# Decode attention with a dense branch on one core: loaded tiles at multiples of 512 bytes, the output sum in four column groups of one bank, and a store in quarter rows

## The chip, the core and the metric

One Trainium2 chip, one of its cores. The metric is the device time in microseconds (us), median of several executions. Executions of one kernel mostly agree within 0.3%, and all that are compared here are of the state "fast" (the one exception, a single look at a kernel that only loads, is marked). The profile's span, from first to last instruction, is about 2 us shorter than the time.

Names in the profiles: PE multiplies matrices and PEld loads its weights; DVE, ACT and POOL are the vector, scalar and general engines; SP issues DMAs (SPq and ACTq are issues by SP and ACT). The inputs lie in HBM, the tiles in SBUF with 128 partitions, the sums of PE in banks of PSUM. The granted clock is the share of full clock that PE was given. A landing is the moment when a DMA's semaphore reports that all of it has arrived.

## The reference, cut to what matters

For two sequences, one token each (`x` is 2x448), the kernel computes `x + attention(layernorm(x)) + mlp(layernorm(x))`.

```python
# attention: 16 query heads, 8 kv heads, head size 256, the last W = 4096 keys of a cache
scores = einsum("bhqd,bhkd->bhqk", q, k[:, :, Sk - W:]) * 256 ** -0.5
o      = einsum("bhqk,bhkd->bhqd", softmax(scores), v[:, :, Sk - W:])   # then @ wo (4096x448)
# mlp: h = xn @ w1 + b1 (448x1792); h * tanh(softplus(h)) @ w2 (1792x448)
```

For each pair of sequence and kv head, 2 MB of K and 2 MB of V are read and used once: 77.66 MB in all with the weights.

## The kernel before: what the change and the argument touch

```python
consts = ctx.enter_context(tc.tile_pool(name="consts", bufs=1))   # small tiles first
wo_pool, k_pool, v_pool, kt_pool = ...                            # 3 x 3,584 B; 4 and 5 x 16,384 B; 3 x 8,192 B a partition
# all the loads below go through one queue, nc.sync, K two heads ahead
nc.sync.dma_start(out=t[:], in_=A_k_cache[b, kvh, s0:Sk, :].rearrange("(p t) d -> p (t d)", p=P))
...
psA = [ps_a.tile([Bsz, DO], FP32, name=f"psA{n}") for n in range(NO)]     # NO = 2 banks, DO = 224
def add(n, lhsT, rhs, **flags):                                          # the sum of all branches
    nc.tensor.matmul(psA[n][:, :], lhsT=lhsT, rhs=rhs, skip_group_check=True, **flags)
...
for n in range(NH):                                                      # softmax denominators, fp32
    nc.tensor.matmul(den[:], lhsT=rs[:, n:n+1].to_broadcast([P, P]), rhs=hsel[:], ...)
...
load_v(i, parts=1 if i < NK - 1 else 2)     # the last V in two halves, then wo in two halves
...
res = consts.tile([Bsz, D], BF16)
nc.vector.tensor_copy(out=res[:, 0:DO], in_=psA[0][:, :])
nc.scalar.copy(out=res[:, DO:D], in_=psA[1][:, :])
nc.sync.dma_start(out=out.flatten_outer_dims(), in_=res[:])
```

After the last V part has landed, `values` multiplies it (a pair of weight load and matmul for each 128x128 block of V), `oT` is scaled, and `mix` multiplies it by wo into `psA`. I call that last `mix` the last product.

The softmax here doesn't subtract the row's maximum and nothing guards it: scores larger than these inputs give would overflow.

## Time and profile before

| | before |
|---|---|
| time | 194.92 us (194.56 to 195.1, 3 runs) |
| span of the profiled run | 192.7 us |
| PE, weight loads, DVE busy | 68%, 42%, 53% of the span |
| read from HBM | 77.67 MB, 403 GB/s over the span |
| last V half lands | 187.2 us |
| from there to the end | 5.5 us |

Read it from the bottom: for 187 us the transfers set the time, then comes a tail that no transfer hides. The prediction below shows the lines.

### The profile page before, as it was taken

The page shows a single profiled execution, that of the slowest core. Times are in us where ns is not written, and L with a number is a line of the kernel's source. Part 1 is how long each engine was busy: PE and PEld are TensorE (multiplying, and loading weights), DVE is VectorE, ACT ScalarE, POOL GpSimd, SP SyncE. Part 2 cuts the span into 40 slices and gives each one's busy share as a digit, 9 for nine tenths or more (in the row PEclk, how much of TensorE's full clock was granted, in tenths as well). Part 3 has the DMA queues.
Part 4 walks back from the last instruction along what each step waited for, and adds up shares of the span by engine and source line. Part 5 has one row for each costly group of instructions (what it writes and reads, how often), then busy time and mean ns, then how long its engine had stood idle before and what let it go on. Part 6 is the DMA issues. An engine that isn't in the chain of part 4 may idle for free.

```text
span 192.7 us, 3810 instructions
## 1 busy us (share of the span) xinstructions
PE 130.4 (68%) x1624; PEld 81.3 (42%) x1624; DVE 102.2 (53%) x137; ACT 25.5 (13%) x69; POOL 24.8 (13%) x138
## 2 busy tenths in 40 slices
PE   0242993999827985499709881797449592898854
PEld 0142381466513654246504651364324452364752
DVE  4605506996638390929264753838091744748101
ACT  5000110112200211012200220021101110021100
POOL 7004320022110112002200210020200200000000
PEclk9999996699995799669975998599957979589965
DMA  6999999999999999999999999999999999999960
GB/s 211 424 447 408 427 427 435 428 435 402 431 422 428 425 415 428 435 418 414 429 425 432 420 416 430 428 425 411 428 432 428 403 434 422 432 414 429 410 253 2
DMA packets 7674, 77.90 MB, mean 404 GB/s; under 512 B 741, under 2 KB 2793, under 8 KB 3050
## 3 DMA queue, kind: packets, MB, share of 16 engines
q1 hardware_dynamic: 7652, 77.66, 96.1%
q8 instruction: 12, 0.20, 0.4%
q14 instruction: 4, 0.03, 0.0%
q10 hardware_dynamic: 6, 0.01, 0.0%
HBM read 77.67 MB, written 0.00 MB: 403 GB/s over the span
## 4 chain that ended last, share of the span: by engine, by line
DMA 96%; PE 1%; SPq 1%; issue 0%; ACT 0%; DVE 0%
DMA v<-in_A_v_cache_dram 51%; DMA k<-in_A_k_cache_dram 18%; DMA wo<-in_A_wo_dram 17%; DMA v<-in_B_w_dram 10%; PE psA L201 1%; PE o L411 1%; SPq L109 0%; SPq L325 0%; ACT res L484 0%; DVE oT L422 0%; SPq L336 0%
## 5 line engine op out<-in xcount | busy, mean ns | idle before, releaser
L352 DVE STREAM_TRANSPOSE kt<-k 128x2048 f32<-128x2048 f32 x32 | 73.5, 2300 | 48.9 <-DMA k<-in_A_k_cache_dram 48.9
L364 PE MATMUL sc<-kt,qdiag 128*128 128x512 bf16 x256 | 75.0, 443 | 14.4 <-DVE kt L352 14.3
L364 PEld LDWEIGHTS <-qdiag 128*128 128x128 bf16 x256 | 26.1, 111 | 50.5 <-issue 24.1
L374 ACT ACTIVATE p<-sc 128x512 bf16<-128x512 f32 x32 | 19.1, 597 | 144.8 <-PE sc L364 140.9
L244 POOL COPY qdiag<-qrep 32x8 bf16<-32x8 bf16 x128 | 21.0, 186 | 125.3 <-PE sc L364 109.8
L201 PE MATMUL psA<-wo,oT 128*2 128x224 bf16 x64 | 12.5, 370 | 31.3 <-DVE oT L422 31.3
L411 PEld LDWEIGHTS <-v 128*128 128x128 bf16 x1024 | 27.9, 97 | 6.3 <-DMA v<-in_A_v_cache_dram 3.0
L411 PE MATMUL o<-pT,v 128*128 128x2 bf16 x1024 | 28.1, 163 | 2.7 <-DMA v<-in_A_v_cache_dram 2.7
L385 DVE STREAM_TRANSPOSE pT<-p 128x512 bf16<-128x512 bf16 x32 | 21.4, 671 | 0.0
L201 PEld LDWEIGHTS <-oT 128*2 128x2 bf16 x64 | 6.5, 111 | 34.6 <-DVE oT L422 32.0
L393 PEld LDWEIGHTS den<-hsel,rs 128*128 128x128 f32 x64 | 11.7, 227 | 3.8 <-issue 2.1
L401 DVE RECIPROCAL rec<-den 128x2 f32<-128x2 f32 x16 | 2.5, 153 | 18.7 <-PE den L393 18.7
L393 PE MATMUL den<-hsel,rs 128*128 128x2 f32 x64 | 9.4, 252 | 0.0
L215 PE MATMUL qT_ps<-xs,v 128*128 128x4 bf16 x112 | 3.3, 166 | 6.1 <-DMA v<-in_A_wq_dram 6.1
L422 DVE TENSOR_TENSOR oT<-o,rec 128x4 bf16<-128x4 f32 x16 | 2.1, 134 | 8.5 <-PE o L411 8.5
L374 ACT ACTIVATION_READ_ACCUMULATOR p<-sc 128x1 f32 x32 | 6.2, 194 | 0.0
L215 PEld LDWEIGHTS <-v 128*128 128x128 bf16 x112 | 3.1, 104 | 6.6 <-DMA v<-in_A_wq_dram 6.6
L224 DVE CAST qT<-qT_ps 128x64 bf16<-128x64 f32 x1 | 0.2, 225 | 7.0 <-PE qT_ps L215 7.0
L169 PE MATMUL xnT_ps<-ident,xn_bf 2*128 2x2 bf16 x7 | 0.5, 166 | 5.0 <-DVE xn_bf L133 5.0
L270 PE MATMUL hT_ps<-xs,v 128*128 128x4 bf16 x49 | 3.7, 195 | 0.0
L270 PEld LDWEIGHTS <-v 128*128 128x128 bf16 x49 | 3.2, 149 | 0.3
L201 PE MATMUL psA<-v,act_bf 128*2 128x224 bf16 x28 | 2.8, 259 | 0.0
(40 smaller groups left out, 22.5 us busy)
## 6 DMA issues: line engine op xcount, KB each, us to landing
k<-in_A_k_cache_dram SPq DMA_DIRECT2D x16, 2048.0 KB, 32.5
v<-in_A_v_cache_dram SPq DMA_DIRECT2D x15, 2048.0 KB, 34.8
v<-in_B_w_dram SPq DMA_DIRECT2D x2, 1568.0 KB, 21.2
wo<-in_A_wo_dram SPq DMA_DIRECT2D x7, 448.0 KB, 31.8
v<-in_A_wq_dram SPq DMA_DIRECT2D x1, 2048.0 KB, 7.8
v<-in_A_v_cache_dram SPq DMA_DIRECT2D x2, 1024.0 KB, 29.9
v<-in_A_wq_dram SPq DMA_DIRECT2D x1, 1536.0 KB, 11.1
wo<-in_A_wo_dram SPq DMA_DIRECT2D x2, 224.0 KB, 24.1
```

The lines of the kernel that those rows point to most:

```text
L201: nc.tensor.matmul(psA[n][:, :], lhsT=lhsT, rhs=rhs, skip_group_check=True, **flags)
L215: nc.tensor.matmul(qT_ps[:, hh, e, :], lhsT=wq_v[s][:, hh, e, :], rhs=xs[:, s, :, :].rearrange("p x b -> p (x b)"), start=(s == 0), stop=( ...
L244: nc.gpsimd.tensor_copy(out=tv[rows, :, e, j * Q : j * Q + rep], in_=qrep[rows, :, h0 : h0 + rep, e, x, b],)
L270: nc.tensor.matmul(hT_ps[:, c, :, :].rearrange("p x b -> p (x b)"), lhsT=w1_v[:, s, c, :], rhs=xs[:, s, :, :].rearrange("p x b -> p (x b)" ...
L352: nc.vector.transpose(out=kt[:].bitcast(FP32), in_=k[:, half * TH * Dh : (half + 1) * TH * Dh].bitcast(FP32),)
L364: nc.tensor.matmul(psc[:], lhsT=qdiag[i % NW][:, n * NE + e, :], rhs=ktv[:, n, e, :, :], start=(n == 0 and e == 0), stop=(n == NB - 1 and ...
L374: nc.scalar.activation(out=p_sb[:], in_=psc[:].rearrange("p t c -> p (t c)"), func=ACT.Exp, scale=scale, accum_out=state["rs", i][:, s % N ...
L385: nc.vector.transpose(out=pT[:], in_=p_t.pop(s)[:])
L393: nc.tensor.matmul(den[:], lhsT=rs[:, n : n + 1].to_broadcast([P, P]), rhs=hsel[:], start=(n == 0), stop=(n == NH - 1),)
L401: nc.vector.reciprocal(out=state["rec", i][:], in_=den[:])
L411: nc.tensor.matmul(po[:, c, :], lhsT=vv[:, t, c, :], rhs=pTv[:, th, 0:rep], start=(t == 0 and c == 0), stop=(t == T - 1), skip_group_check ...
L422: nc.vector.tensor_tensor(out=oT[:, :, :, b], in0=po[:], in1=state.pop(("rec", i))[:].unsqueeze(1).to_broadcast([P, ND, rep]), op=ALU.mult,)
```

## The change

It has four parts. (1) The big pools stand right after two small tiles (`hsel` is widened for it) that together end at a multiple of 512 bytes, so every loaded tile starts at a multiple of 512 in its partition instead of at 96 modulo 256. The aim is cheaper transfers. (2) The sum runs in four column groups of 32 columns of the PE array, each with a quarter of the 448 output columns, in one bank; one copy takes it out; two queues store it as quarter rows. The aim is a shorter tail. (3) The denominators use a constant matrix of ones, after two small DVE instructions. (4) The last V comes as a half and two quarters.

```diff
-    consts = ctx.enter_context(tc.tile_pool(name="consts", bufs=1))
+    lead = ctx.enter_context(tc.tile_pool(name="lead", bufs=1))
+    ident = lead.tile([P, P], BF16)
+    hsel = lead.tile([P, Q], FP32)
     wo_pool = ...   # k_pool, v_pool, kt_pool
+    consts = ctx.enter_context(tc.tile_pool(name="consts", bufs=1))
@@
-    psA = [ps_a.tile([Bsz, DO], FP32, name=f"psA{n}") for n in range(NO)]   # NO = 2
+    psA = ps_a.tile([P, DO], FP32, name="psA")                              # NO = 4, DO = 112
+    def add(lhsT, w, start=False, stop=False):
+        for n in range(NO):
+            nc.tensor.matmul(psA[n * Q : n * Q + Bsz, :], lhsT=lhsT,
+                rhs=w[:, n * DO : (n + 1) * DO], start=start, stop=stop,
+                tile_position=(0, n * Q), skip_group_check=True)
@@
-        for n in range(NH):
-            nc.tensor.matmul(den[:], lhsT=rs[:, n : n + 1].to_broadcast([P, P]), rhs=hsel[:], ...)
+        nc.vector.tensor_scalar(out=sums[:], in0=hsel, scalar1=rs[:, 0:1], ...)
+        nc.vector.scalar_tensor_tensor(out=sums[:], in0=hsel, scalar=rs[:, 1:2], in1=sums[:], ...)
+        nc.tensor.matmul(den[:], lhsT=ones_f[:], rhs=sums[:], start=True, stop=True)
@@
-            load_v(i, parts=1 if i < NK - 1 else 2)
+            load_v(i, (0, T) if i < NK - 1 else (0, T // 2, 3 * T // 4, T))
@@
-    res = consts.tile([Bsz, D], BF16)
-    nc.vector.tensor_copy(out=res[:, 0:DO], in_=psA[0][:, :])
-    nc.scalar.copy(out=res[:, DO:D], in_=psA[1][:, :])
-    nc.sync.dma_start(out=out.flatten_outer_dims(), in_=res[:])
+    res = consts.tile([P, DO], BF16)
+    nc.vector.tensor_copy(out=res[:], in_=psA[:])
+    for b, queue in zip(range(Bsz), (nc.sync, nc.scalar)):
+        queue.dma_start(out=out[b].rearrange("s (n d) -> (s n) d", n=NO), in_=res[b : P : Q, :])
```

More of the change, by code (lines that the diff above doesn't have):

```diff
@@ L110 @@
         wq_sb += [w[:, s, :] for s in range(hi - lo)]
-    ident = consts.tile([P, P], BF16)
     make_identity(nc, ident[:])
@@ L152 @@
             )
-    hsel = consts.tile([P, rep], FP32)
-    nc.vector.tensor_copy(out=hsel[:], in_=ident[:, 0:rep])
+    hsel = hsel[:, 0:rep]
+    nc.vector.tensor_copy(out=hsel, in_=ident[:, 0:rep])
     for j in range(1, NQ):
         nc.vector.tensor_tensor(
-            out=hsel[:], in0=hsel[:], in1=ident[:, j * Q : j * Q + rep], op=ALU.add
+            out=hsel, in0=hsel, in1=ident[:, j * Q : j * Q + rep], op=ALU.add
         )
+    ones_f = consts.tile([P, P], FP32)
+    nc.gpsimd.memset(ones_f[:], 1.0)
     NW = 3
@@ L193 @@
     nc.vector.memset(ones[:], 1.0)
-    NO = 2
+    NO = NQ
     DO = D // NO
-    psA = [ps_a.tile([Bsz, DO], FP32, name=f"psA{n}") for n in range(NO)]
-    def add(n, lhsT, rhs, **flags):
-        nc.tensor.matmul(psA[n][:, :], lhsT=lhsT, rhs=rhs, skip_group_check=True, **flags)
-    for n in range(NO):
-        add(n, ident[0:Bsz, 0:Bsz], x_bf[:, n * DO : (n + 1) * DO], start=True, stop=False)
+    psA = ps_a.tile([P, DO], FP32, name="psA")
+    def add(lhsT, w, start=False, stop=False):
+        for n in range(NO):
+            nc.tensor.matmul(
+                psA[n * Q : n * Q + Bsz, :],
+                lhsT=lhsT,
+                rhs=w[:, n * DO : (n + 1) * DO],
+                start=start,
+                stop=stop,
+                tile_position=(0, n * Q),
+                skip_group_check=True,
+            )
+    nc.vector.memset(psA[:], 0.0)
+    add(ident[0:Bsz, 0:Bsz], x_bf[:, :], start=True)
     qrep = consts.tile([P, NB, HH, NE, NX, Bsz], BF16)
@@ L307, in dense_out @@
             for c in range(NF):
-                for n in range(NO):
-                    add(
-                        n,
-                        act_bf[:, c, x, :],
-                        w2_sb[:, x, c, n * DO : (n + 1) * DO],
-                        start=False,
-                        stop=False,
-                    )
+                add(act_bf[:, c, x, :], w2_sb[:, x, c, :])
     NSTEP = len(heads) * NH
@@ L328, in load_k, with load_v @@
         k_t[i] = t
-    def load_v(i, parts=1):
+    def load_v(i, cuts=(0, T)):
         kvh, b = heads[i]
@@ L333, in load_v @@
         vin = A_v_cache[b, kvh, s0:Sk, :].rearrange("(p t) d -> p t d", p=P)
-        for u in range(parts):
-            ts = slice(u * T // parts, (u + 1) * T // parts)
-            nc.sync.dma_start(out=t[:, ts, :], in_=vin[:, ts, :])
+        for lo, hi in zip(cuts, cuts[1:]):
+            nc.sync.dma_start(out=t[:, lo:hi, :], in_=vin[:, lo:hi, :])
         v_t[i] = t
@@ L390, in turn_p @@
         rs = state.pop(("rs", i))
-        den = ps_den.tile([P, rep], FP32, tag="den", name="den")
-        for n in range(NH):
-            nc.tensor.matmul(
-                den[:],
-                lhsT=rs[:, n : n + 1].to_broadcast([P, P]),
-                rhs=hsel[:],
-                start=(n == 0),
-                stop=(n == NH - 1),
-            )
+        sums = small.tile([P, rep], FP32, tag="sums", name="sums")
+        nc.vector.tensor_scalar(
+            out=sums[:], in0=hsel, scalar1=rs[:, 0:1], scalar2=None, op0=ALU.mult
+        )
+        nc.vector.scalar_tensor_tensor(
+            out=sums[:], in0=hsel, scalar=rs[:, 1:2], in1=sums[:], op0=ALU.mult, op1=ALU.add
+        )
+        den = ps_den.tile([P, rep], FP32, tag="den", name="den")
+        nc.tensor.matmul(den[:], lhsT=ones_f[:], rhs=sums[:], start=True, stop=True)
         state["rec", i] = small.tile([P, rep], FP32, tag="rec", name="rec", bufs=4)
@@ L432, in mix @@
         for h in range(rep):
-            for n in range(NO):
-                for c in range(ND):
-                    add(
-                        n,
-                        oT[:, c, h, :],
-                        w[:, h, c * D + n * DO : c * D + (n + 1) * DO],
-                        start=False,
-                        stop=(kvh == Hkv - 1 and h == rep - 1 and c == ND - 1),
-                    )
+            for c in range(ND):
+                add(
+                    oT[:, c, h, :],
+                    w[:, h, c * D : (c + 1) * D],
+                    stop=(kvh == Hkv - 1 and h == rep - 1 and c == ND - 1),
+                )
     NK = len(heads)
@@ L480 @@
                 mix(kvh)
-    res = consts.tile([Bsz, D], BF16)
-    nc.vector.tensor_copy(out=res[:, 0:DO], in_=psA[0][:, :])
-    nc.scalar.copy(out=res[:, DO:D], in_=psA[1][:, :])
-    nc.sync.dma_start(out=out.flatten_outer_dims(), in_=res[:])
+    res = consts.tile([P, DO], BF16)
+    nc.vector.tensor_copy(out=res[:], in_=psA[:])
+    for b, queue in zip(range(Bsz), (nc.sync, nc.scalar)):
+        queue.dma_start(
+            out=out[b].rearrange("s (n d) -> (s n) d", n=NO), in_=res[b : P : Q, :]
+        )
     issue_in_order(tc)
```

## The prediction

> **What bounds the kernel now.** I began with the page's second part, because it shows at once whether an engine or the transfers fill the span.
>
> ```profile
> PE   0242993999827985499709881797449592898854
> DMA  6999999999999999999999999999999999999960
> GB/s 211 424 447 408 427 427 435 428 435 402 431 422 428 425 415 428 435 418 414 429 425 432 420 416 430 428 425 411 428 432 428 403 434 422 432 414 429 410 253 2
> ```
>
> From the second slice on the DMA digit never leaves 9 until the two last slices, while PE falls to 2 and 4. A stretch of the middle puts a number on it:
>
> ```profile
> 30.00:180.00 150.00, 108.65 (x1272) 65.53 (x1272) 89.66 (x95) 20.88 (x61) 15.86 (x96) 0.83 1.01 424
> ```
>
> The columns are the stretch, PE, PEld, DVE, ACT and POOL busy us, the granted clock, the DMA share and GB/s. DMA share 1.01 means that no DMA engine pauses (neighbouring packets overlap a little); PE is busy 72% of the stretch, DVE 60%. So work on PE or DVE in the middle lies beside the transfers. Then the chain of waits, in order of time:
>
> ```profile
> 156.59 30.62 DMA v<-in_A_v_cache_dram
> 187.21 0.05 issue
> 187.26 1.02 PE o L411 x32
> ...
> 188.31 0.18 DVE oT L422
> ...
> 188.53 1.67 PE psA L201 x8
> ...
> 190.22 0.34 ACT res L484
> ```
>
> Before 187.2 us the chain is transfers alone; after the last V half has landed come 5.5 us (192.7 - 187.2) that no transfer hides. The time can therefore change in two places only: the rate of a stream of 77.66 MB, and this tail. The tail in detail, from the timeline:
>
> ```profile
> 187.26 1.01 PE L411 MATMUL o<-pT,v 128*128 128x2 bf16 x32 [1.47 <-DMA v<-in_A_v_cache_dram]
> 188.53 1.65 PE L201 MATMUL psA<-wo,oT 128*2 128x224 bf16 x8 [0.26 <-DVE oT L422]
> 189.84 0.38 DVE L483 CAST res<-psA 2x224 bf16<-2x224 f32 x1 [1.37 <-PE psA L201]
> 190.22 0.34 ACT L484 CAST res<-psA 2x224 bf16<-2x224 f32 x1 [11.00 <-PE psA L201]
> 190.58 0.34 SPq L485 DMA_DIRECT2D out_dram<-res  x1
> ```
>
> The reader should see that the ACT copy starts only when the second bank is complete, so it stands wholly on the path. One more landing matters, that of wo, which the last product needs:
>
> ```profile
> L345 SPq DMA_DIRECT2D wo<-in_A_wo_dram x9: 328/379/379, 17.2 to 166.4; - x9
> DMA to landing us min/median/max: 21.9/31.8/34.0
> ```
>
> The last issue is at 166.4; the last one having the shortest time to landing, it lands at 166.4 + 21.9 = 188.3, only 0.2 us before the product starts at 188.5. The semaphore records of the landings agree: the two wo halves land at 187.77 and 188.33.
>
> **What the Trainium skill says.** "DMA: Bandwidth & Descriptors", section "How a descriptor splits into AXI transactions", says that transactions start at multiples of 256 B and that a descriptor starting elsewhere pays beats of 32 B for bytes that it does not use. In the program as built, every K, V and wo tile starts at 96 modulo 256; in the changed one, at 0. If the rule cost full price on the written side, it would be 96/32 = 3 beats per row. The section "Where 436 GB/s comes from" of the same page gives 32 B at 850 MHz for each of 16 ports. The packet records of this trace fit that: by size, the commonest duration is 74 ns for 1,792 B, 239 for 6,272, 460 for 12,288, 469 for 12,544, 612 for 16,384. Subtract 56, 196, 384, 392 and 512 beats at 1.176 ns and 8 to 10 ns are left in each. The telling packet is the load of the bias, 3,584 B to a tile that already starts at a multiple of 256: 140 ns, less 112 beats (131.8) = 8 ns, the same. So this trace does not show the three beats in a misaligned row. "TensorEngine Tiling (Array Packing)", section "Key Properties", says that tiles of the array work independently and in parallel, but that changing the tiling mode drains the engine; the kernel before uses no tiles, so its trace shows neither. "Issuing engines are not separate DMA queues", again on the DMA page, says that two issuers save only issue time; here one issue took 0.34 us.
>
> **The change part by part.**
>
> *Alignment.* The stream cannot gain more than what is left over in a packet: about 9 of 612 ns, 1.5%, or 2.7 us of the 185 us between first and last landing. The full three beats would be 3.5/612 = 0.6%, 1.1 us. The aligned bias packet speaks for nothing, so I put in 0.1 us.
>
> *Mid-kernel work.* The sum of the branches goes from 2 x 47 = 94 products of 224 columns (64 + 28 + 2 on PE) to 188 of 112; the denominators from 64 fp32 passes to about 32 (-10 us of PE and of weight loads together, half of 9.4 + 11.7), with 32 more small DVE instructions, at about 0.14 us each (the 128x4 and 128x2 ones take 134 and 153 ns) +4.5 us of DVE. PE at 72% and DVE at 60% have room: 0 on the path. PE's net increase in instructions may cost one more 16 KB instruction fetch on a DMA engine, 0.6 us on one of 16: 0.1 us.
>
> *V in a half and two quarters.* After the last landing, 16 pairs instead of 32. Their spacing is (1.01 - 0.17)/31 = 27 ns, so 16 x 27 = 0.43 us go. The product could start at 188.1. wo's first half (187.77) is there; the second half (188.33) is needed only after eight of the new matmuls.
>
> *The last product.* Before: 8 matmuls, latency 0.39, spacing (1.65 - 0.39)/7 = 0.18 us, about what 224 columns take at the granted clock of 0.5 here. After: 16 of 112 columns. Run one by one they take 16 x 0.09 + 0.3 = 1.75 us: nothing gained. With four column groups at once, only issue is left, which I estimate by the 27 to 32 ns of the V pairs: 16 x 0.032 + 0.3 = 0.8 us, ending at 188.1 + 0.8 = 188.9 and just after wo's last landing plus its eight matmuls (188.33 + 0.26 + 0.3). Before it ended at 190.2. I choose a point short of full overlap, 1.05 us: it ends near 189.15. With the V part that is 1.05 us saved.
>
> *Copy and store.* One DVE copy of 112 columns in place of the two. The DVE copies from PSUM to bf16 took 225 ns for 64 columns (qT) and 379 for 224 (res), 0.96 ns a column, so 271 ns stand where the ACT copy's 335 and its gap stood: 0.1 us saved. The store sends rows of 224 B on two queues instead of 896 B on one; two issues run side by side, and the ACT issue at the start took 0.54 against 0.34 here. I book 0.1 us lost. The rest of the tail, about 2 us from issue to end, stays.
>
> Sum: -0.1 (alignment) + 0.1 (fetch) - 1.05 - 0.1 + 0.1 = -1.05 us; with some weight for a partial gain of the stream, -1.3 us, 194.92 - 1.3 = 193.6 us, 0.7% less.
>
> **The rivals.**
>
> *Alignment does matter.* The records could hide a cost on the written side, which the single aligned packet, alone on one row at the start, would not show under load. For it: 424 GB/s is below 435. Against: a rate of 612 + 9/8 ns for each 16,384 B row (a 9 ns semaphore packet after eight rows) gives 427 GB/s, and the smaller wo rows and fetches explain the rest. At its price of 3 beats: 192.6; with all 9 ns gone: 190.9.
>
> *wo becomes the bound.* If the stream's end moves later by another order of packets, the product waits for the second wo half however fast V is done. The margin is 0.2 us before; after, the earliest end is 188.33 + 0.6. If the column groups also do not overlap, the product saves only 0.3 us: 194.5.
>
> *Drains and the small store eat the tail.* Each change between whole-array and column-group work may drain PE, and short HBM writes may land later. Nothing in the trace prices either. At 0.3 us each: 194.2. A loss of 2% would need 3.9 us, most of the tail again; I see nothing of that size.
>
> **Range and chances.** The tail alone spans 0.3 to 1.7 us, giving 193.2 to 194.6; a stream gain of 1 us more lowers it to 192.2. The three runs before differ by 0.5 us. So 192.1 to 194.7. Faster by over 2% means below 191.0: 2.7 + 1.2 us, nearly all that both places could give at once: 4%. Slower by 2%: 1%.
>
> **What would show it.** Right: DMA share and about 424 GB/s in 30 to 180 us unchanged, 16,384 B packets still at 612 ns, the last V landing within 0.5 us of 187.2; the last product in about 1 us or less, one copy of 0.27 us, a tail from the V landing of about 4.4 us. Wrong on alignment: packets near 603 to 608 ns and an earlier V landing. Wrong on the groups: the last product still 1.6 us or more. Wrong on wo: a pause inside the last product, ended by wo's landing.

## The result, and the profile after

The changed kernel took 192.71 us (median of 4 runs, 192.62 to 193.02), against 194.75 for the kernel before (4 runs): ratio 0.9896, 95% interval 0.9876 to 0.9917. A ratio is the mean time of one kernel's runs over that of the other's in the same rounds, so it is not quite the ratio of the medians quoted.

First the same stretch of the middle as before, with the same columns (the last two are the DMA share and GB/s):

```profile
30.00:180.00 150.00, 108.31 (x1318) 57.55 (x1318) 95.60 (x127) 20.89 (x61) 15.87 (x96) 0.78 1.01 428
```

The DMA share is still 1.01, but 428 GB/s are moved in place of 424. Then the end of the chain of waits:

```profile
160.12 25.71 DMA v<-in_A_v_cache_dram
185.83 0.05 issue
185.87 0.60 PE o L418 x16
...
186.50 0.18 DVE oT L429
...
186.72 0.61 PE psA L208 x16
```

The last V lands at 185.83, not 187.21, and the last product takes 0.61 us, not 1.67. The end of the timeline shows copy and stores (start, duration, engine, line):

```profile
187.35 0.27 DVE L487 CAST res<-psA 128x112 bf16<-128x112 f32 x1 [0.69 <-PE psA L208]
187.66 0.65 SPq L489 DMA_DIRECT2D out_dram<-res  x1
187.66 0.61 ACTq L489 DMA_DIRECT2D out_dram<-res  x1
```

The copy is as short as foreseen, but each store takes 0.6 us to issue where the one before took 0.34, and the end comes 3.14 us after the issue began (190.8 - 187.66) instead of 2.14 (192.72 - 190.58). The longer issue is only 0.3 us of that: by the semaphore records the last landing comes 1.17 instead of 0.81 us after the issue has ended, and the end of the span 1.35 instead of 0.99 us after that landing. The change of the span, by stretches:

| stretch | before | after | change | predicted |
|---|---|---|---|---|
| to the last V landing | 187.21 | 185.83 | -1.38 | 0.0 (-0.1 alignment, +0.1 fetch) |
| landing to start of last product | 1.32 | 0.89 | -0.43 | -0.43 |
| last product | 1.67 | 0.61 | -1.06 | -0.62 |
| its end to the issue of the store | 0.38 | 0.33 | -0.05 | -0.1 |
| issue to end | 2.14 | 3.14 | +1.00 | +0.1 |
| sum | 192.7 | 190.8 | -1.9 | -1.05 |

So two large terms that the prediction had near zero, the stream and the store, go in opposite directions. The experiments test both.

### The profile page after: what moved, and what is told of

Its sections match the earlier page's. It is cut to its first block, busy times and chain, and to the rows that moved or that the text cites. A ratio compares the mean times of both kernels' runs of the same rounds, so it can differ in the third digit from the quotient of the medians.

```text
span 190.8 us, 3941 instructions
## 1 busy us (share of the span) xinstructions
PE 128.5 (67%) x1686; PEld 72.5 (38%) x1686; DVE 108.5 (57%) x170; ACT 25.1 (13%) x68; POOL 25.0 (13%) x139
## 4 chain that ended last, share of the span: by engine, by line
DMA 93%; DVE 3%; PE 1%; SPq 0%; issue 0%
DMA k<-in_A_k_cache_dram 62%; DMA wo<-in_A_wo_dram 18%; DMA v<-in_A_v_cache_dram 13%; DVE kt L359 2%; DVE pT L392 1%; SPq L113 0%; PE psA L208 0%; PE o L418 0%; DVE res L487 0%; DVE oT L429 0%; DVE sums L399 0%; DVE sums L402 0%; SPq L333 0%
## 5 line engine op out<-in xcount | busy, mean ns | idle before, releaser
L371 PE MATMUL sc<-kt,qdiag 128*128 128x512 bf16 x256 | 85.9, 494 | 13.2 <-DVE kt L359 13.2
L371 PEld LDWEIGHTS <-qdiag 128*128 128x128 bf16 x256 | 29.3, 123 | 54.4 <-issue 37.3
L208 PE MATMUL psA<-wo,oT 128*2 128x112 bf16 x128 | 4.2, 276 | 23.5 <-DVE oT L429 23.5
L406 PEld LDWEIGHTS den<-sums,ones_f 128*128 128x128 f32 x32 | 7.2, 252 | 18.4 <-DVE sums L402 17.8
L406 PE MATMUL den<-sums,ones_f 128*128 128x2 f32 x32 | 6.7, 280 | 9.7 <-DVE sums L402 9.7
L208 PEld LDWEIGHTS <-oT 128*2 128x2 bf16 x128 | 2.2, 98 | 24.3 <-DVE oT L429 24.2
L402 DVE SCALAR_TENSOR_TENSOR sums<-hsel,rs,sums 128x2 f32<-128x2 f32 x16 | 3.5, 220 | 0.6
```

The costliest lines, as they stand in the source:

```text
L208: nc.tensor.matmul(psA[n * Q : n * Q + Bsz, :], lhsT=lhsT, rhs=w[:, n * DO : (n + 1) * DO], start=start, stop=stop, tile_position=(0, n * ...
L371: nc.tensor.matmul(psc[:], lhsT=qdiag[i % NW][:, n * NE + e, :], rhs=ktv[:, n, e, :, :], start=(n == 0 and e == 0), stop=(n == NB - 1 and ...
L402: nc.vector.scalar_tensor_tensor(out=sums[:], in0=hsel, scalar=rs[:, 1:2], in1=sums[:], op0=ALU.mult, op1=ALU.add)
L406: nc.tensor.matmul(den[:], lhsT=ones_f[:], rhs=sums[:], start=True, stop=True)
```

## The experiments

### Where the tiles start

Is it the start address that made the stream faster? Four variants of the changed kernel have a filler of 32, 96, 128 or 256 bytes behind `hsel`, which moves every loaded tile. In the expectations, "the page" and the beat are those of "DMA: Bandwidth & Descriptors", section "How a descriptor splits into AXI transactions", of the Trainium skill, as the prediction has them.

```diff
     hsel = lead.tile([P, Q], FP32)
+    shift = lead.tile([P, 48], BF16)      # 96 bytes; 16, 64 and 128 columns for the others
```

> The changed kernel with every loaded tile moved to 96 modulo 512, where the kernel before had them (96 modulo 256). Theory A, the start address prices a packet: the packets of 16,384 B spread again over 611 to 620 ns (mean near 615 without the few over 700) and the last V landing moves from 185.8 back to about 187.2 us; time 1.3 to 1.5 us over the changed kernel, near 194.1. Theory B, the stream got faster through something else (denominators, column groups, order of the pools): packets stay at 611 and the time stays at 192.7.

> Tiles at 32 modulo 512. If the price is one beat of 1.18 ns for each 32 B of start (A1): packets of 16,384 B in steps of about 1.2 ns, 611 to 614, mean near 612.5, V landing near 186.2, time near 193.1. If any misaligned row pays the same (A2): mean near 615 as at 96, time near 194.1.

> Tiles at 128 modulo 512. A1 (price by the distance from a multiple of 256): steps of 4 beats, 4.7 ns, packets at 611, 616 and 620, mean near 616.5, V landing near 187.6, time near 194.5. A2: mean near 615, time near 194.1. A third, that multiples of 64 or 128 suffice: all at 611 and 192.7.

> Tiles at 256 modulo 512. If 256 is the granule, as the page has it for reads: all packets at 611, time 192.7. If the 512 of the change is needed: a spread and a time of 193.5 or more.

And the other way round, the kernel before with a filler in front of its big pools and nothing else changed:

```diff
+    shift = ctx.enter_context(tc.tile_pool(name="shift", bufs=1)).tile([P, 80], BF16)
     wo_pool = ctx.enter_context(tc.tile_pool(name="wo", bufs=3))
```

> The kernel before with a 160 B filler ahead of the loaded tiles, so that these start at multiples of 512 and nothing else changes. If alignment alone makes the faster stream: packets of 16,384 B at 611, last V landing at 185.8, tail as before (5.5 us), time 193.3 (-1.4 us, ratio 0.993). If the stream's gain needs the other parts: time 194.7 and packets of 611 to 620.

Measured (the mean is that of the 16,384 B packets that start after 20 us and take less than 640 ns; the few longer ones are counted apart; "V ends" is the end of the last packet of V in us):

```
kernel     start mod 512   mean ns   over 640   V ends   time us   ratio (95% interval)
before          352         614.6      108      186.7     194.7    1
off96            96         614.5      118      186.9     194.58   1.0005 (0.9985 to 1.0025)
off32            32         615.8      109      187.3     194.98   1.0012 (0.9998 to 1.0027)
off128          128         614.3      115      187.1     195.12   1.0024 (1.0001 to 1.0048)
off256          256         611.0       13      185.4     193.36   0.9930 (0.9907 to 0.9952)
b_align           0         611.0       12      185.3     192.98   0.9915 (0.9901 to 0.9929)
changed           0         611.0       11      185.4     192.71   0.9896 (0.9876 to 0.9917)
```

The stretch from 30 to 180 us of off96 and then of b_align shows the rate in the last column:

```profile
30.00:180.00 150.00, 104.49 (x1254) 55.59 (x1255) 95.49 (x125) 20.20 (x59) 15.84 (x96) 0.80 1.01 424
```

```profile
30.00:180.00 150.00, 107.44 (x1276) 64.67 (x1277) 90.36 (x97) 20.86 (x61) 15.84 (x96) 0.83 1.01 428
```

Theory A holds from both sides: moving the tiles back to 96 takes the whole gain away, and alignment alone makes the kernel before 1.65 us faster (0.85%). Theory B falls. In the aligned kernels about 99% of the packets take exactly 611 ns; in the misaligned ones they spread, in the kernel before over clusters at 611 to 612, 615 and 619, in off32 mostly at 614 and 621. The packets account for the whole gain: all packets of the load queue from 19.5 us on, added up and divided by 16 engines, take 167.3 us in the kernel before and in off96, and 165.9 us in the changed kernel and in b_align. Of these 1.4 us, 0.84 are the 3.6 ns on each of the 3,732 packets in the mean; the rest is mostly in the longer packets (108 over 640 ns against 11) and in the rows of wo (76.4 against 74.5 ns). 256 is enough for the packets, so the 512 of the change is not needed for them. The time of off256 is less clear: its four runs go from 192.54 (the profiled one) to 193.89, and why the later ones are slower no profile shows.

A1, a price by the distance from the multiple of 256, falls too: 32 costs at least as much as 96 or 128. All three misaligned starts that were tried pay a similar price, 3.3 to 4.8 ns in the mean.

off96 lost more than the 1.4 us that I had put on the stream (194.58 against 192.71). In its profiled run, one of its faster ones (span 192.4, against 190.8 of the changed kernel), V ends 1.5 us later, which is nearly all of that run's difference; its runs spread from 194.21 to 195.47, and what the slower ones add no profile shows.

### Are the engines to blame for the slow packets?

The spread might come from PE and DVE using SBUF beside the transfers. This variant of the kernel before only loads; its tiles still start at 96 modulo 256 (a filler keeps them there). Its output is wrong, which doesn't matter for the time. The edit in words:

```diff
-    project(); build_q(0); build_q(1); turn(0) and, in the loop, turn, scores, turn_p, build_q, dense_in, dense_out, values, mix
+    res = consts.tile([Bsz, D], BF16)
+    nc.vector.tensor_copy(out=res[:], in_=v_t[NK - 1][0:Bsz, T - 2 : T, 0:DO])
     nc.sync.dma_start(out=out.flatten_outer_dims(), in_=res[:])
```

> Loads alone, wrong result on purpose: the kernel before without scores, values and products, tiles at 96 modulo 256 as before. If the misaligned packets are slowed by what the engines do with SBUF beside them: all packets of 16,384 B at 611 ns and the stream at 428 GB/s. If it is a matter of the packets themselves: the same spread of 611, 615 and 619 as in the kernel before, and 424 GB/s.

One look gave 188.94 us (a single run, its state unknown). In the middle no engine works:

```profile
30.00:180.00 150.00, 0.00 (x0) 0.00 (x0) 0.00 (x0) 0.00 (x0) 0.00 (x0) 1.00 1.01 425
```

Yet the mean packet is 614.7 ns, with the same clusters (870 packets at 612, 842 at 615, 583 at 619). It is a matter of the packets themselves. The stream ends 2.5 us earlier all the same (last V packet at 184.2 against 186.7 us), so the rest of the kernel does cost the stream something, by another way than the length of the common packet; by which, this run does not separate. The run shows something else: the spread has a beginning. In this kernel, in the kernel before and in off96, packets between 10 and 15 us take 611 ns although their rows start at 96, and all rows of the first weights take one duration (460 ns for 12,288 B, but for one packet in off96). The spread begins with the load of w2, from 19.5 us on, the first large load whose source rows (6,272 B) are no multiple of 256 long. In the changed kernel the same load is followed by no spread (all later packets of its kind at 239 ns). What happens in the DMA engines at that load, and why it lasts, no run here settles.

### The store

Three variants of the end of the changed kernel. First, the sum is copied back into two full rows and stored by one DMA (two DVE copies beside two ACT copies):

```diff
-    res = consts.tile([P, DO], BF16); one copy; two stores of quarter rows
+    res = consts.tile([Bsz, D], BF16)
+    for n in range(NO):
+        dst, src = res[:, n * DO : (n + 1) * DO], psA[n * Q : n * Q + Bsz, :]
+        if n % 2: nc.scalar.copy(out=dst, in_=src)
+        else: nc.vector.tensor_copy(out=dst, in_=src)
+    nc.sync.dma_start(out=out.flatten_outer_dims(), in_=res[:])
```

> The changed kernel with the sum copied by two DVE and two ACT copies of 2x112 into one [2, 448] tile, stored by one DMA as before. If the two stores of quarter rows cost the 1.0 us that the trace shows between issue and end (3.14 against 2.14 us): copies 0.2 us longer, store 1.0 us shorter, time near 191.9. If the longer end has another cause (the later engines' shutdown): 192.7 to 192.9.

Second, both quarter-row stores on one queue, `(nc.sync, nc.sync)` for `(nc.sync, nc.scalar)`:

> The changed kernel with both quarter-row stores on the SP queue. If two queues issuing at the same moment slow each other (0.61 and 0.65 us instead of 0.34): each issue takes about 0.35 us, one after the other, time within 0.1 us of 192.7. If a store of four short rows is slow by itself: two issues of 0.6 us in a row, time near 193.3.

The end of the timeline of a_onestore, then of a_onequeue:

```profile
187.22 0.56 DVE L492 CAST res<-psA 2x112 bf16<-2x112 f32 x2 [0.69 <-PE psA L208]
187.25 0.51 ACT L490 CAST res<-psA 2x112 bf16<-2x112 f32 x2 [7.55 <-PE psA L208]
187.86 0.33 SPq L493 DMA_DIRECT2D out_dram<-res  x1
```

```profile
187.50 1.21 SPq L489 DMA_DIRECT2D out_dram<-res  x2
```

a_onestore took 191.87 us, ratio 0.9853 (0.9839 to 0.9866), as expected: the copies are 0.29 us longer, but from issue to end it is 190.1 - 187.86 = 2.2 us again. This version beats both kernels. a_onequeue took 192.78 us, ratio 0.9900 (0.9887 to 0.9914), the same as the changed kernel. Its two issues take 1.21/2 = 0.6 us each with nothing beside them, so contention between two queues is not the cause: a store of four rows of 224 B, read from partitions 32 apart, costs 0.6 us to issue, one of two rows of 896 B 0.33. Whether the number, the length or the partitions of the rows make it, no variant separates. My time for that outcome (193.3) was too high, since the second issue in a row moved the last landing of the store only from 189.48 to 189.74 us by the semaphore records.

### The quarters of V, and a pause

The changed kernel with the last V in halves again, `(0, T // 2, T)`:

> The changed kernel with the last V in two halves. By the working of the prediction 16 more pairs at 27 to 29 ns after the last landing: +0.43 us, time near 193.1. If the second half of wo sets the start of the last product anyway: less than 0.2 us.

It took 192.84 us, ratio 0.9905 (0.9891 to 0.9919): 0.2 us over the changed kernel at most, and the intervals overlap. The reason that I had put beside it, wo, is not the one: in the profiled run its second half landed at 186.57, and the last product started at 187.61. Why so little of the 0.43 shows is not settled. The last V part landed 0.19 us earlier than in the changed kernel (185.64 against 185.83), which takes back part of the 0.43. And the profiled run is the slowest of the five (193.40; the others 192.67 to 192.87), so it does not speak for them. In it PE sits idle inside the last head at 185.4 us, with the first half of V, which it works on, landed since 183.0, and nothing released it. The same pause is in the changed kernel. The weight loads on PE near the end, changed kernel:

```profile
181.20 2.59 PEld L418 LDWEIGHTS <-v 128*128 128x128 bf16 x85
184.35 0.80 PEld L418 LDWEIGHTS <-v 128*128 128x128 bf16 x27 [0.56 <-issue]
185.87 0.51 PEld L418 LDWEIGHTS <-v 128*128 128x128 bf16 x16 [0.73 <-DMA v<-in_A_v_cache_dram]
```

Of the 85 pairs, 64 belong to the head before; so PE stops after pair 21 of the last head, for "issue", which means that the profile shows no wait. It then does 11 pairs, to the end of the first half, and 16 for the first quarter, and only the last 16 wait for V.

My theory was the fetch of instructions. "Runtime: NRT & Kernel Launch", section "Instruction fetch mechanics", in the Trainium skill says that an engine's instructions come in blocks of 16 KiB (256 instructions), fetched by a DMA while the block before is executed, and that the cost is mostly hidden. The trace agrees on the blocks: 13 packets of 16,384 B on the instruction queue after the change, 12 before. All eight profiled kernels with four groups and without the extra pairs below stop after the same pair 21, and in all eight the pause ends 2.3 to 2.6 us after the last but one such packet starts (181.96 to 184.35 in the changed kernel). To test it, ten needless transposes were put at the start of PE's program in the single-store variant:

```diff
-    for s in range(NS):
+    for s in [0] * 10 + list(range(NS)):
         nc.tensor.transpose(xnT_ps[:, s, :], ...)
```

> The single-store variant with ten needless PE transposes (10 pairs) at the start, result unchanged. Theory F: the pause of PE inside the last head, after pair 21, with no releaser in the profile, is a wait for the next block of instructions, so it depends on the count of PE instructions alone: it moves to pair 11 of that head. Theory G, the pause is a wait for V or for the transposed scores: it stays at pair 21. Time 191.8 to 192.0 either way.

The weight loads of a_onestore, then of a_fetch:

```profile
182.14 2.53 PEld L418 LDWEIGHTS <-v 128*128 128x128 bf16 x85
185.02 1.23 PEld L418 LDWEIGHTS <-v 128*128 128x128 bf16 x43 [0.35 <-issue]
```

```profile
182.00 2.26 PEld L418 LDWEIGHTS <-v 128*128 128x128 bf16 x75
184.68 1.49 PEld L418 LDWEIGHTS <-v 128*128 128x128 bf16 x53 [0.42 <-issue]
```

85 becomes 75: the pause moved by exactly the ten pairs, to pair 11. Theory F holds and G falls. The time stayed at 191.88 us, ratio 0.9869 (0.9848 to 0.9890). Where PE gets to this block late, the pause outlasts the landing of the last V part (a_halves resumes at 186.04 after 185.64, off32 at 188.31 after 187.95); where it gets there early, V comes later and the pause is free, as in the changed kernel's profile.

What makes PE late shows in these two runs, both the slowest of their kernels (193.40 and 195.93 us). Their last product starts 1.97 and 1.93 us after the last V landing (0.89 in the changed kernel), and the chain that ended last leaves the transfers at the last landing of K (169.8 and 171.7 us) and runs through DVE and PE to the end. The last scores are where it loses time, here in the changed kernel, then in a_halves:

```profile
176.33 1.90 PE L371 MATMUL sc<-kt,qdiag 128*128 128x512 bf16 x8
176.42 3.57 PE L371 MATMUL sc<-kt,qdiag 128*128 128x512 bf16 x8
```

The granted clock was 1.00 in the first stretch and 0.50 in the second (off32: 3.57 us at 0.50). a_wide, below, had the slow scores too but no pause, and its product started 0.89 us after V. Slow scores and the pause together go with the late end; no run changes the clock alone. Part (3) puts two small DVE instructions on this chain, and no variant takes part (3) back alone: what it costs in such a run is not shown.

### The column groups

The changed kernel with the sum, the copies and the store as before (two banks, 224 columns, no column groups):

> The changed kernel with the sum made as before: two banks, 224 columns, no column groups, two copies, one store; alignment, denominators and V quarters stay. It has 94 pairs fewer on PE. If the column groups are worth what the traces say, the last product takes 1.65 us instead of 0.6 and the time is about 0.7 us over the single-store variant (191.87), near 192.6. If the product gains nothing on the path because PE waits elsewhere, it is 191.9 to 192.1.

And two column groups of 224 columns in one bank, one DVE and one ACT copy side by side, one store (in a_onestore, `NO = 2` instead of `NO = NQ`):

> A version meant to be best: two column groups of 224 columns in one bank, one DVE and one ACT copy side by side, one store. Last product 8 matmuls, about 0.8 us if two groups overlap (1.65 if not); copies 0.38 instead of 0.56 us; store as before. If they overlap: 191.7 to 191.9; if not: 192.5.

The last product in a_wide, then in a_two:

```profile
186.73 1.65 PE L208 MATMUL psA<-wo,oT 128*2 128x224 bf16 x8 [0.26 <-DVE oT L427]
```

```profile
186.37 0.91 PE L208 MATMUL psA<-wo,oT 128*2 128x224 bf16 x8 [0.26 <-DVE oT L429]
```

a_wide took 192.81 us, ratio 0.9901 (0.9887 to 0.9916): against a_onestore (0.9853), the groups with their copies are worth 0.9 us. Its product is 1.05 us longer, its copies up to the issue 0.27 us shorter (0.40 against 0.67). a_two took 191.86 us, ratio 0.9861 (0.9847 to 0.9876), the same as four groups: its product is 0.3 us longer, its copies 0.18 us shorter. The granted clock was 0.50 during the last product in all four kernels (before, changed, a_wide, a_two), so the clock is not the reason. In a_two PE runs through the 64 + 48 pairs without the pause; it has 94 pairs fewer ahead.

## Why the prediction was right or wrong, point by point

The time, 192.71 us, lies in the stated range, 0.9 us below 193.6; the saving was 2.0 us instead of 1.3. That the sum came out so near is partly luck: the stream and the product gave 1.4 and 0.4 us more than booked, and the store took back 0.9.

- **What bounds the kernel** was right: the stream to the last V landing and the tail behind it account for all of the change in the profiled runs. The extra work of DVE (102.2 to 108.5 us busy, 6.3 where 4.5 were foreseen) is not on the chain of the changed kernel's profile; in those of off32 and a_halves it is, and it was not tested alone.
- **Alignment** was wrong, and this is the step that failed: "The aligned bias packet speaks for nothing, so I put in 0.1 us." b_align measured 1.65 us. The comparison took commonest durations; the 612 of the kernel before and the 611 after differ by next to nothing there too. The price is in the rest of the distribution, which I did not write down: a mean of 614.6 ns, with clusters at 615 and 619. And the bias packet came in at the start, in a part of the run where misaligned rows show no price either; in the changed kernel its tile starts at 128 modulo 256, by the addresses of the built program, and the packet again took 140 ns. The other signs did turn: 428 GB/s instead of an unchanged 424, and the last V landing 1.4 us earlier; the packets at 603 to 608 ns that were to show it never came. The first rival named this very weakness ("alone on one row at the start, would not show under load") and should have had more weight; that its price of 3 beats, 3.5 ns a packet, comes close to the 3.6 ns found (614.6 - 611.0) is luck, since a start one beat past the multiple (off32) costs 4.8 and one four beats past it (off128) 3.3.
- **V in a half and two quarters** was right by the trace of the changed kernel (-0.43 us), but a_halves shows at most 0.2 us of it in the time, and why so little is not settled. What the 0.1 us for one more instruction fetch left out is that PE itself waits for the block; I had only counted the packet on a DMA engine.
- **The last product** had the right mechanism and was too cautious in size: 0.61 us, even below the 0.8 of full overlap. The term that was mis-sized is the issue: the sixteen matmuls start within 0.29 us, four at a time about 3 ns apart, where 16 x 0.032 = 0.51 was booked; the last one then takes the 0.3 as foreseen. No drain shows: it starts 0.04 us after `oT`, as before, and wo's second half, landed at 186.91 by the semaphore records, did not hold it up.
- **The copy** was right: 0.27 us.
- **The store** was mis-sized: +0.1 us predicted, +1.0 measured. The rival "drains and the small store eat the tail" had 0.3 for it. a_onestore gets 0.84 us of it back in the time. The prediction priced only the issue; the later landing and the later end after it, 0.36 us each, it had at nothing.

With the tiles back at 96, all the other parts together are worth nothing measurable (off96: 1.0005): the 1.0 us of the store stands against the 1.5 us that product and quarters gave in the profile, and the rest goes in a stream that ended 0.2 us later and in the spread of its runs.

## What to carry to other kernels

In a kernel bound by loads, check where each loaded tile starts in its partition and put it at a multiple of 256 bytes; here that alone gave 0.85%, and it cost a filler of 160 bytes. When judging a cost per packet, compare whole distributions, under load, and not the commonest value. After any change of a tail, look at the issue and landing of the last store as closely as at the compute ahead of it, and if an engine pauses there for no reason that the profile names, count its instructions against the blocks in which they are fetched.

## What the Trainium skill lacked or had wrong

- "DMA: Bandwidth & Descriptors", "How a descriptor splits into AXI transactions": the granule of 256 B agrees (over 99% of the packets at 611 ns for starts of 0 and 256 modulo 512), but the page prices only a start in beats proportional to its distance. For destinations in SBUF the runs show a price that does not grow with the distance (means of 615.8, 614.5 and 614.3 ns at 32, 96 and 128), and none between 10 us and the load with source rows of 6,272 B that began at 19.5 us.
- The same page, "Issuing engines are not separate DMA queues", says that a second issuing engine saves only issue time: agreed (192.71 us with two queues, 192.78 with one). That a store of four rows of 224 B costs 0.6 us to issue where one of two rows of 896 B costs 0.33 stands on none of the pages I read.
- "TensorEngine Tiling (Array Packing)", "Key Properties": column groups do run in parallel (16 matmuls of 112 columns in 0.61 us against 8 of 224 in 1.65), and the drain at a change of mode that the page warns of shows no cost here.
- "Runtime: NRT & Kernel Launch", "Instruction fetch mechanics": "mostly hidden" did not hold among pairs of weight load and matmul of 27 to 30 ns: PE paused 0.35 to 1.0 us (at no cost where V came later still), and the new block was usable 2.3 to 2.6 us after its packet started on DMA engines that were full of loads.
